# First loads of a four-block transformer kernel on three queues, with its written-out orders replaced

## The chip, the cores and the metric

The kernel runs on one core of a Trainium2 chip. The core has five engines that work side by side and wait for each other on semaphores: PE (TensorE, matrix products), DVE (VectorE), ACT (ScalarE), POOL (GpSimd) and SP (SyncE, which here only issues transfers). Transfers can be issued by SP, ACT and POOL, each through a queue of its own. The metric is the device time of one execution in microseconds (us). The kernel before takes 323.23 us, the median of three runs (323.01 to 323.62).

## The reference, cut to what matters

The input x has 2048 rows of 512 bf16 values. Two kinds of block alternate, A, B, A, B, each added to its input:

```
phi(t) = where(t > 0, t + 1, exp(t)) + 1e-6
A(x): y = layernorm(x);  q, k, v = y @ wqkv              # 32 heads of 16
      kv = sum over rows of phi(k)^T v ;  z = sum over rows of phi(k)
      o  = (phi(q) kv) / (phi(q) z + 1e-6) ;  return o @ wo
B(x): y = layernorm(layernorm(x))
      return gelu(y @ w1 + b1) @ w2 + b2                  # 512 -> 1792 -> 512
x = x + A(x);  x = x + B(x);  x = x + A(x);  x = x + B(x)
```

Because kv and z are sums over all rows, no output of a block A can be formed before every row has passed through its k product.

## The kernel before

The 2048 rows are 16 tiles of 128 rows, in four chunks of four. Operations carry names: layer (0 or 1), then tile or chunk. `K0_3` is the k product of tile 3 in layer 0 (four matmuls of 512 columns); `G0_3` adds (normalised x)^T phi(k) of that tile into four held PSUM banks; `Q0_0_2` is the q product for chunk 0; `Z` sums phi(k); `KV`, `M` and `WO` make the block's output; `W1x` and `W2x` are the two products of block B.

A tile passes through these steps in the first block A. DVE takes statistics (`statsA0_3`, `aggrA0_3`), POOL makes the inverse deviation (`vepsA0_3`, `powA0_3`, a power of -0.5), DVE or ACT normalises (`normA0_3`). The result is transposed so that PE can multiply it by the weights: by a transposing DMA on SP (`TA0_3`), or, for the tiles at the very start, by PE against an identity (`PTA0_3`) and a copy out of PSUM by ACT (`tcA0_3`). Tiles 0 and 1 use a shortened way: only the mean is taken off (`cenA0_0`), PE transposes that (`PTC0`, `tcC0`), and the missing scale is applied where ACT reads the k product (`expk0_0`, `reluk0_0`). Tile 3 gets its statistics from ACT (`sumA0_3`, `sqA0_3`, with a small step `negA0_3` on POOL). After the k product, ACT takes exp and relu of it, DVE a minimum (`mink0_0`) and a sum (`phik0_0`); that is phi(k).

Nothing is ordered by the hardware or a planner at run time. The table `CONF` (L241 to L606) holds for every engine the list of all its operations by name (`ORDER`), the buffer of every tile (`PLACES`), the engine of each operation that has a choice (`WAY`), the first loads (`LOADS`), and a train of matmuls on constants that PE plays while no data is there (`WARM`: seven of 512 columns in `warm0`, eight of 256 columns in `warm1` to `warm8`). Each engine plays its list strictly in order (L1306 to L1318). An operation that waits holds up all that is behind it on the same engine, transfers issued by that engine included. `ACT` loads its function table first (L1310).

The lists begin so (before):

```
sp:   x0 x1 wka wkc xc1 wq xc3 TA0_0 TA0_1 xc2 TA0_5 TA0_4 TA0_7 TA0_6 ...
act:  wkb wkd sumA0_3 tcC0 sqA0_3 tcC1 reluk0_0 tcA0_2 expk0_0 tcA0_3 expk0_1 reluk0_1 ...
pool: id0 neghalf bdm0 bdm1 id1 vepsA0_0 powA0_0 negA0_3 vepsA0_2 powA0_2 vepsA0_3 powA0_3 ...
dve:  ones statsA0_0 aggrA0_0 cenA0_0 statsA0_2 statsA0_1 ... normA0_2 statsA0_5 normA0_3 aggrA0_5 normA0_1 statsA0_4 mink0_0 ...
pe:   warm0 warm8 warm2 warm6 PTC0 warm1 warm7 warm5 warm4 warm3 K0_0a K0_0b PTC1 K0_0c K0_0d PTA0_2 K0_1 PTA0_3 K0_2 K0_3 G0_0_0 G0_1_0 Q0_0_2 ...
```

`x0` is tile 0 (128 KB), `x1` tiles 1 to 3 (384 KB), `xc1` to `xc3` the other chunks (512 KB each; `xc1` is issued only when `x0` has landed), `wka` to `wkd` the four quarters of the key weights (128 KB each; rows 0-127, 256-383, 128-255 and 384-511 are wka, wkb, wkc and wkd), `wq` the query weights (512 KB). `wkb` waits for `ones`, a DVE memset. `K0_0` is split in four matmuls, each needing one quarter of the key weights, in the order 2, 0, 3, 1 (`ks0`, used at L874 to L883). `bdm0`, `bdm1` and `id1` build a mask and the identity on POOL. The value weights and the weights of block B are issued by POOL much later (`wv`, `wo`, `w1_0` ... at L728), after all `TA0` transposes have landed.

Of the kernel before, what the change touches and what calls it, by code (L numbers as in the profile page):

```python
# [1359 lines left out]
```

## Time and profile before

| | |
|---|---|
| median of three runs | 323.23 us (323.01 to 323.62) |
| the profiled execution | 323.1 us, of which 321.9 us lie between its first and last instruction (the span) |
| PE busy | 318.0 us of the span, granted clock 1.00 |
| DVE, ACT, POOL busy | 218.1, 189.3 and 145.5 us |
| first transfer issued | 0.79 us after the start of the span |
| x0 landed, statistics of tile 0 begin | 3.25 us |
| last idle time of PE before the end | ends at 9.16 us |

Times in the text are us from the start of the span unless said otherwise. "Busy" for PE counts a matmul from its start until its result has drained, so a few tenths of waiting can hide inside a busy share; the starts in the timeline show them. A run of matmuls of 512 columns starts one every 0.216 us (four of them: 0.86 us). In the timeline a line is `start, duration, engine, source line, operation, out<-in, count`, and what stands in brackets is the engine's idle time before it and what ended it. A "q" behind an engine's name marks the transfers that it issues.

### The profile page before, as it was taken

Reading aid. Unit: us, or ns where it says so; the run is one execution under the profiler, and the core shown is the slowest. Engines: PE = TensorE matmul, PEld = TensorE weight load, DVE = VectorE, ACT = ScalarE, POOL = GpSimd, SP = SyncE. Lnnn points to the kernel's source line nnn. Section 1 sums busy time; section 2 is a strip of 40 time slices with the busy share of each in tenths; the row PEclk is TensorE's granted clock in tenths of the full one; section 3 lists DMA queues with packets and bytes.
Section 4 is the critical chain, followed back from the end, with each engine's and each line's share of the span. In section 5 each row is a group of like instructions: output and inputs, shape, how many; then the busy total and the mean of one; then the engine's idle time right before and its main releaser. Section 6 shows DMA issues by size and latency. Waiting matters only on the chain.

```text
span 321.9 us, 4748 instructions
## 1 busy us (share of the span) xinstructions
PE 318.0 (99%) x1703; PEld 157.4 (49%) x1703; DVE 218.1 (68%) x529; ACT 189.3 (59%) x324; POOL 145.5 (45%) x216
## 2 busy tenths in 40 slices
PE   8999999999999999999999999999999999999997
PEld 3444554666444444444444444558544444444444
DVE  5998789999786774028848899999889881101103
ACT  5898656797730636667962367979634442663320
POOL 6573978688655355101822415887454163000000
DMA  7844793142121412111010200122232322201002
GB/s 257 200 81 85 241 348 85 35 82 36 33 49 34 82 33 51 34 33 32 18 40 10 51 16 0 35 51 52 50 62 54 98 65 67 49 0 35 16 33 65
DMA packets 52355, 21.68 MB, mean 67 GB/s; under 512 B 47532, under 2 KB 50860, under 8 KB 52332
## 3 DMA queue, kind: packets, MB, share of 16 engines
q1 hardware_dynamic: 50844, 16.37, 22.4%
q0 software_dynamic: 1056, 4.72, 4.3%
q10 hardware_dynamic: 432, 0.30, 0.3%
q8 instruction: 13, 0.21, 0.3%
q14 instruction: 10, 0.08, 0.1%
HBM read 8.00 MB, written 2.10 MB: 31 GB/s over the span
## 4 chain that ended last, share of the span: by engine, by line
PE 97%; DMA 2%; DVE 0%; issue 0%
PE ps L1153 30%; PE ps L1190 29%; PE ps L1123 9%; PE ps L879 8%; PE ps L896 6%; PE ps L984 4%; PE ps L1013 4%; DMA t<-in_A_x_dram 2%; PE ps L909 2%; PE ps L1176 1%; PE ps L970 1%; PE ps L1034 1%; PE ps L1057 1%; PE ps L1100 1%; DVE stats L775 0%; PE ps L1048 0%
## 5 line engine op out<-in xcount | busy, mean ns | idle before, releaser
L1158 ACT ACTIVATE gT<-ps,b1c 128x512 bf16<-128x512 f32 (+1 forms) x140 | 77.0, 601 | 68.7 <-PE ps L1153 68.1
L1153 PE MATMUL ps<-t,w 128*128 128x512 bf16 (+1 forms) x560 | 102.5, 336 | 0.0
L1190 PE MATMUL ps<-w,gT 128*128 128x512 bf16 x434 | 98.6, 379 | 0.0
L1153 PEld LDWEIGHTS ps<-t,w 128*128 128x128 bf16 x560 | 54.8, 98 | 43.7 <-ACT gT L1158 0.2
L1190 PEld LDWEIGHTS ps<-w,gT 128*128 128x128 bf16 x434 | 42.5, 98 | 50.4
L784 POOL TENSOR_TENSOR rstd<-veps,neghalf 128x1 f32<-128x1 f32 x64 | 39.0, 625 | 41.1 <-DVE veps L782 38.9
L847 ACT ACTIVATE eb<-ps 128x512 bf16<-128x512 f32 x62 | 35.4, 606 | 19.3 <-PE ps L896 7.3
L1200 DVE TENSOR_TENSOR yb<-ps,xsb 128x512 bf16<-128x512 f32 x15 | 10.2, 688 | 41.4 <-PE ps L1190 41.4
L775 DVE BATCH_NORM_STATS2 stats<-xsb 128x6 f32<-128x512 f32 x48 | 32.0, 681 | 0.3
L1123 PE MATMUL ps<-gtb,t 128*128 128x512 bf16 x128 | 31.4, 379 | 0.0
L879 PE MATMUL ps<-wqkv,t 128*128 128x512 bf16 x128 | 30.9, 379 | 0.3 <-ACT t L835 0.3
L858 ACT ACTIVATE rb<-ps 128x512 bf16<-128x512 f32 x43 | 25.3, 607 | 5.8 <-PE ps L879 5.8
L798 ACT ACTIVATE yb<-xsb,nmr,rstd 128x512 bf16<-128x512 f32 x21 | 16.9, 814 | 15.1 <-POOL nmr L795 15.1
L896 PE MATMUL ps<-wqkv,t 128*128 128x512 bf16 x96 | 24.1, 379 | 0.0
L1089 POOL TENSOR_TENSOR t<-t,rr 128x512 bf16<-128x512 bf16 x18 | 19.3, 1072 | 9.0 <-DVE rr L1085 6.4
L782 POOL TENSOR_SCALAR veps<-mv 128x1 f32<-128x1 f32 x35 | 8.2, 236 | 32.7 <-DVE mv L777 31.3
L1196 DVE TENSOR_TENSOR xsb<-ps,xsb 128x512 f32<-128x512 f32 x16 | 10.8, 678 | 17.9 <-PE ps L1190 17.9
L1139 POOL TENSOR_TENSOR xsb<-xsb,b2b 128x512 f32<-128x512 f32 x17 | 21.4, 1267 | 3.0 <-DVE yb L803 2.9
L1077 POOL TENSOR_TENSOR lr<-t,zrow 128x512 f32<-128x512 bf16 x14 | 16.5, 1179 | 7.3 <-ACT zrow L997 4.5
L1123 PEld LDWEIGHTS ps<-gtb,t 128*128 128x128 bf16 x128 | 12.5, 98 | 14.5
L803 DVE TENSOR_SCALAR yb<-xsb,mv,rstd 128x512 bf16<-128x512 f32 x27 | 14.5, 542 | 7.3 <-POOL rstd L784 6.0
L879 PEld LDWEIGHTS ps<-wqkv,t 128*128 128x128 bf16 x128 | 12.1, 98 | 14.7 <-ACT t L835 0.9
(99 smaller groups left out, 363.7 us busy)
## 6 DMA issues: line engine op xcount, KB each, us to landing
w<-in_B_w_dram POOLq DMA_DIRECT2D x4, 896.0 KB, 9.1
out_dram<-yb SPq DMA_DIRECT2D x15, 128.0 KB, 2.0
t<-in_A_x_dram SPq DMA_DIRECT2D x3, 512.0 KB, 4.8
t<-yb SPq DMA_TRANSPOSE x62, 2.5
wqkv<-in_A_wqkv_dram SPq DMA_DIRECT2D x1, 512.0 KB, 5.9
wqkv<-in_A_wqkv_dram POOLq DMA_DIRECT2D x1, 512.0 KB, 4.7
wo<-in_A_wo_dram POOLq DMA_DIRECT2D x1, 512.0 KB, 5.3
t<-in_A_x_dram SPq DMA_DIRECT2D x1, 384.0 KB, 3.3
```

Source lines behind the costliest of these rows:

```text
L775: G.op("dve", lambda e: e.bn_stats(stats[:, s.slot, :], src()), 620, reads=src_keys, writes=[k + "s"], tiles=[s, *src_tiles], name=f"stats ...
L784: G.op("pool", lambda e: e.tensor_tensor(rstd[:, s.slot:s.slot + 1], veps[:, s.slot:s.slot + 1], neghalf[:], op=ALU.pow), 570, reads=[k + ...
L847: G.op("act", lambda e: e.activation(eb[:, et.slot, :], bank(bt), ACT.Exp, scale=by()), 478, reads=[src_key, *more_keys], writes=[f"e{tag} ...
L858: G.op("act", lambda e: e.activation(rb[:, rt.slot, :], bank(bt), ACT.Relu, scale=by()), 478, reads=[src_key, *more_keys], writes=[f"r{tag ...
L879: ins = e.matmul(bank(b), lhsT=yTa(yT)[:, dt, k * P:(k + 1) * P], rhs=wqkv[:, dt, D:2 * D], start=(i == 0 and n == 0), stop=(i == len(part ...
L896: ins = e.matmul(bank(b), lhsT=yTa(yT)[:, dt, k * P:(k + 1) * P], rhs=wqkv[:, dt, 0:D], start=(dt == 0), stop=(dt == DT - 1))
L1089: lambda e, d=d, tok=tok, heads=heads: e.tensor_tensor(heads(tok()), heads(tok()), rr[:, d.slot, :].unsqueeze(2).broadcast_to([P, H, DH]), ...
L1123: ins = e.matmul(bank(wb), lhsT=yTa(pq)[:, kt, k * P:(k + 1) * P], rhs=gtb[:, kt, :], start=(kt == 0), stop=(kt == DT - 1))
L1139: G.op("pool" if on_pool else "dve", lambda e: e.tensor_tensor(xsb[:, st, :], xsb[:, st, :], b2b[:], op=ALU.add), 1120 if on_pool else 600 ...
L1153: ins = e.matmul(bank(b, n), lhsT=w1[:, dt, ft * P:(ft + 1) * P], rhs=yTa(yT)[:, dt, k0 * P:k1 * P], start=(dt == 0), stop=(dt == DT - 1))
L1158: G.op("act", lambda e, ft=ft, b=b, k0=k0, k1=k1, n=n: e.activation(gT[:, g.slot, ft * 512 + k0 * P:ft * 512 + k1 * P], bank(b, n), ACT.Ge ...
L1190: ins = e.matmul(bank(b), lhsT=gT[:, g.slot, ft * 512 + k * P:ft * 512 + (k + 1) * P], rhs=w2[:, ft, :], start=(ft == 0), stop=(ft == FT - 1))
```

## The change

Three things change in `CONF`; the arithmetic, the number of operations on PE and their sizes stay, but for `K0_0`.

First, the loads. `x1` moves from SP to ACT, where it is the first instruction behind the table load and waits for nothing. The key weights come as three transfers: `wkb` (quarter 0, SP), `wka` (quarter 1, ACT) and `wkp` (quarters 2 and 3 in one transfer of 256 KB, POOL, between `id1` and `vepsA0_0`). `K0_0` is now three steps: `K0_0a` needs wkb, `K0_0b` needs wka, and `K0_0c`, two matmuls, needs wkp.

Second, the lists of all engines are new from the start to about the first block's output, and again in the second block A and the start of the second block B (`Q1_...` to `W11_0_...`). The middle and the tail are as before. Third, buffers are placed anew to fit (PSUM banks, `t4`, statistics slots), and seven small steps change engine: `b21_4` and `pr1_3_3` from POOL to DVE, `vepsA0_13` and `vepsB1_6` from POOL to DVE, `vepsB0_7`, `vepsB1_1` and `vepsB1_5` from DVE to POOL.

```diff
-    LOADS=[['x0', 'sp', 'x', 0, 0, 1, ''], ['x1', 'sp', 'x', 0, 1, 4, ''], ['wkb', 'act', 'wk', 0, 2, 3, 'ones'], ['wka', 'sp', 'wk', 0, 0, 1, ''], ['wkd', 'act', 'wk', 0, 3, 4, ''], ['wkc', 'sp', 'wk', 0, 1, 2, ''], ['xc1', 'sp', 'x', 1, 0, 4, 'x0'], ['wq', 'sp', 'wq', 0, 0, 4, ''], ['xc3', 'sp', 'x', 3, 0, 4, ''], ['xc2', 'sp', 'x', 2, 0, 4, '']],
+    LOADS=[['x0', 'sp', 'x', 0, 0, 1, ''], ['x1', 'act', 'x', 0, 1, 4, ''], ['wkb', 'sp', 'wk', 0, 0, 1, ''], ['wka', 'act', 'wk', 0, 1, 2, ''], ['wkp', 'pool', 'wk', 0, 2, 4, ''], ['xc1', 'sp', 'x', 1, 0, 4, 'x0'], ['wq', 'sp', 'wq', 0, 0, 4, ''], ['xc3', 'sp', 'x', 3, 0, 4, ''], ['xc2', 'sp', 'x', 2, 0, 4, '']],
         "sp":
-            "x0 x1 wka wkc xc1 wq xc3 TA0_0 TA0_1 xc2 TA0_5 TA0_4 TA0_7 TA0_6 TA0_13 TA0_14 TA0_15 TA0_12 TA0_8 TA0_10 TA0_9 "
+            "x0 wkb xc1 wq xc3 TA0_0 TA0_1 TA0_5 TA0_4 xc2 TA0_7 TA0_6 TA0_13 TA0_14 TA0_12 TA0_8 TA0_15 TA0_10 TA0_9 TA0_11 "
         "pe":
-            "warm0 warm8 warm2 warm6 PTC0 warm1 warm7 warm5 warm4 warm3 K0_0a K0_0b PTC1 K0_0c K0_0d PTA0_2 K0_1 PTA0_3 K0_2 "
-            "K0_3 G0_0_0 G0_1_0 Q0_0_2 Q0_0_1 Q0_0_0 K0_5 G0_2_0 K0_4 Z0_0 G0_3_0 Q0_1_0 K0_7 Q0_1_3 K0_6 G0_4_0 G0_5_0 "
+            "warm0 warm2 warm7 warm6 PTC0 warm4 warm3 warm1 warm5 K0_0a K0_0b warm8 PTC1 K0_0c PTA0_2 K0_1 PTA0_3 K0_2 G0_0_0 "
+            "K0_3 G0_1_0 Q0_0_2 Q0_0_1 Q0_0_0 K0_5 K0_4 G0_2_0 Q0_1_0 K0_7 G0_3_0 Q0_1_3 G0_4_0 Z0_0 K0_6 Q0_1_2 G0_5_0 K0_14 "
         "act":
-            "wkb wkd sumA0_3 tcC0 sqA0_3 tcC1 reluk0_0 tcA0_2 expk0_0 tcA0_3 expk0_1 reluk0_1 reluk0_3 expk0_2 reluk0_2 "
+            "x1 wka sumA0_3 tcC0 sqA0_3 tcC1 expk0_0 tcA0_2 reluk0_0 expk0_1 tcA0_3 reluk0_1 expk0_2 reluk0_3 reluk0_2 "
         "dve":
-            "statsA0_5 normA0_3 aggrA0_5 normA0_1 statsA0_4 mink0_0 aggrA0_4 phik0_0 mink0_1 normA0_5 phik0_1 statsA0_7 "
+            "statsA0_5 normA0_3 aggrA0_5 mink0_0 normA0_1 phik0_0 statsA0_4 mink0_1 aggrA0_4 normA0_5 phik0_1 statsA0_7 "
         "pool":
-            "id0 neghalf bdm0 bdm1 id1 vepsA0_0 powA0_0 negA0_3 vepsA0_2 powA0_2 vepsA0_3 powA0_3 powA0_1 vepsA0_5 powA0_5 "
+            "id0 neghalf eps6 bdm0 bdm1 id1 wkp vepsA0_0 negA0_3 powA0_0 b1z vepsA0_2 powA0_2 vepsA0_3 powA0_3 powA0_1 "
...
-            "nmrA0_10 vepsA0_9 powA0_9 nmrA0_11 phik0_14 eps6 wv wo phik0_8 w1_0 w1_1 w2_0 w2_1 phiq0_1_1 pr0_0_0 pz0_1_0 "
+            "vepsA0_9 nmrA0_10 nmrA0_11 powA0_9 phik0_14 wv phik0_8 wo phiq0_1_1 w1_0 w1_1 w2_0 w2_1 pr0_0_0 pz0_1_0 pr0_0_3 "
...
-        "den0_3": "tok", "den1_1": "tok", "den1_2": "tok", "den1_3": "tok", "ks0": "2|0|3|1", "normA0_0": "dve",
+        "den0_3": "tok", "den1_1": "tok", "den1_2": "tok", "den1_3": "tok", "ks0": "0|1|23", "normA0_0": "dve",
```

Functions gain the choice of other chunk orders (`CHUNKS`) and of a half-and-half way of the denominator (`by_half`, `load_half`); with the table as given the chunk order is 0, 1, 2, 3 everywhere and no entry asks for the half way, so these branches make the same instructions as before.

More of the change, by code (lines that the diff above doesn't have):

```diff
@@ L709, in load_w, with load_half @@
                                [f"{which}_{d}" for d in range(d0, d1)], name=name, kb=128 * (d1 - d0), after=after)
+        def load_half(name, queue, h, after):
+            G.parts[("x0", 0)] = (("x0", 0, 0), ("x0", 0, 1))
+            ps_ = slice(64 * h, 64 * h + 64)
+            loaded[name] = dma(queue, lambda e: e.dma_start(
+                t4[ps_, x0[0].slot, 0:D].rearrange("p (k d) -> p k d", k=1), rows(x_dram, 0)[ps_, 0:1, :]),
+                [("x0", 0, h)], [x0[0]], name=name, kb=64, after=after)
         for name, queue, what, at, lo, hi, behind in cf["LOADS"]:
             after = [loaded[b] for b in behind.split()]
-            if what == "x":
+            if what == "half":
+                load_half(name, queue, at, after)
+            elif what == "x":
                 load_x(name, queue, at, lo, hi, after)
@@ L751, in build_kernel, with by_token, by_half @@
             G.op("pe", warm, sum(cols) / 1.2, tiles=[wu], name=f"warm{n}", n=len(cols))
-        def by_token(L, c):
-            return eng(f"den{L}_{c}") == "tok"
+        def by_token(L, c, k=0):
+            way = eng(f"den{L}_{c}")
+            return way == "tok" or (way == "half" and k >= 2)
+        def by_half(L, c):
+            return eng(f"den{L}_{c}") == "half"
+        tokq = {}
         def norm(src, src_keys, src_tiles, double, on_act, tag, src16=False, head=False, centred=None):
@@ L862, in phi @@
             on_pool = eng(f"phi{tag}") == "pool"
             G.op("pool" if on_pool else "dve",
-                 lambda e: e.tensor_tensor(dst(), eb[:, et.slot, :], rb[:, rt.slot, :], op=ALU.add),
-                 1150 if on_pool else 338, reads=[f"e{tag}", f"r{tag}"], writes=[dst_key], tiles=[et, rt, *dst_tiles],
+                 lambda e: e.tensor_tensor(dst(), eb[:, et.slot, 0:n], rb[:, rt.slot, 0:n], op=ALU.add),
+                 (1150 if n == D else 580) if on_pool else (338 if n == D else 190), reads=[f"e{tag}", f"r{tag}"], writes=[dst_key], tiles=[et, rt, *dst_tiles],
@@ L887, in attn_q, with fn @@
         def attn_q(L, c, yT, pq):
-            if by_token(L, c):
-                for k in range(4):
+            half = by_half(L, c)
+            own = pq
+            if half:
+                own = tokq[(L, c)] = Tile(T4, f"pqt{L}_{c}")
+            n = 2 * P if half else 4 * P
+            if not by_token(L, c):
+                for kt in range(DT):
+                    b = Tile(psum, f"q{L}_{c}_{kt}" + "c" * half, "q")
+                    def fn(e, kt=kt, b=b):
+                        for dt in range(DT):
+                            ins = e.matmul(bank(b, n), lhsT=wqkv[:, dt, kt * P:(kt + 1) * P], rhs=yTa(yT)[:, dt, 0:n],
+                                           start=(dt == 0), stop=(dt == DT - 1))
+                        return ins
+                    G.op("pe", fn, 4 * MM if n == D else 4 * (n / 2.4 + 2.5), reads=[f"yT{L}_{4 * c + k}" for k in range(n // P)] + ["wq"], writes=[f"q{L}_{c}_{kt}" + "c" * half],
+                         tiles=[b, yT], name=f"Q{L}_{c}_{kt}" + "c" * half, lat=MM_DRAIN, n=4)
+                    phi(b, f"q{L}_{c}_{kt}" + "c" * half, lambda kt=kt: yTa(pq)[:, kt, 0:n], f"pq{L}_{c}_{kt}" + "c" * half, [pq], f"q{L}_{c}_{kt}" + "c" * half, n=n)
+            for k in range(4):
+                if by_token(L, c, k):
                     b = Tile(psum, f"q{L}_{c}_{k}", "q")
@@ L900, in attn_q, with attn_z @@
                          tiles=[b, yT], name=f"Q{L}_{c}_{k}", lat=MM_DRAIN, n=4)
-                    phi(b, f"q{L}_{c}_{k}", lambda k=k: t4[:, pq.slot, k * D:(k + 1) * D], f"pq{L}_{c}_{k}", [pq],
+                    phi(b, f"q{L}_{c}_{k}", lambda k=k: t4[:, own.slot, k * D:(k + 1) * D], f"pq{L}_{c}_{k}", [own],
                         f"q{L}_{c}_{k}")
-                return
-            for kt in range(DT):
-                b = Tile(psum, f"q{L}_{c}_{kt}", "q")
-                def fn(e, kt=kt, b=b):
-                    for dt in range(DT):
-                        ins = e.matmul(bank(b), lhsT=wqkv[:, dt, kt * P:(kt + 1) * P], rhs=yTa(yT)[:, dt, :],
-                                       start=(dt == 0), stop=(dt == DT - 1))
-                    return ins
-                G.op("pe", fn, 4 * MM, reads=[f"yT{L}_{4 * c + k}" for k in range(4)] + ["wq"], writes=[f"q{L}_{c}_{kt}"],
-                     tiles=[b, yT], name=f"Q{L}_{c}_{kt}", lat=MM_DRAIN, n=4)
-                phi(b, f"q{L}_{c}_{kt}", lambda kt=kt: yTa(pq)[:, kt, :], f"pq{L}_{c}_{kt}", [pq], f"q{L}_{c}_{kt}")
         zfirst = {}
-        def attn_z(L, c, pks):
-            by_sum = [int(v) for v in (eng("zc0") or "").split()] if L == 0 else list(range(NC - 1))
+        def attn_z(L, c, pks, order):
+            by_sum = [int(v) for v in (eng("zc0") or "").split()] if L == 0 else order[:NC - 1]
+            others = [v for v in order if v not in by_sum]
             def fold(add):
@@ L973, in attn_z, with attn_g_held @@
             G.op("pe", fn, 400, reads=[f"pk{L}_{4 * c + k}" for k in range(4)] + ["onesm"], writes=[f"zc{L}_{c}"], tiles=[b, *pks], name=f"Z{L}_{c}", lat=MM_DRAIN, n=16)
-            total(b, f"zc{L}_{c}", f"zs{L}_{c}", bool(L) or c != min(v for v in range(NC) if v not in by_sum))
-            if L == 0 and by_sum and c == max(v for v in range(NC) if v not in by_sum):
+            total(b, f"zc{L}_{c}", f"zs{L}_{c}", bool(L) or c != others[0])
+            if L == 0 and by_sum and c == others[-1]:
                 fold(True)
-        def attn_g_held(L, st, k, y, ykey, pk, gb):
-            parts = [(dc,) for dc in range(DT)] if st == ST - 1 else [tuple(range(DT))]
+        def attn_g_held(L, st, k, y, ykey, pk, gb, first, last):
+            parts = [(dc,) for dc in range(DT)] if last else [tuple(range(DT))]
             for part in parts:
@@ L984, in fn @@
                         ins = e.matmul(ps[:, gb.slot + dc, :], lhsT=yb[:, y.slot, dc * P:(dc + 1) * P], rhs=pkb[:, pk.slot, :],
-                                       start=(st == 0), stop=(st == ST - 1))
+                                       start=first, stop=last)
                     return ins
                 keys = [f"g{L}_{dc}" for dc in part]
-                G.op("pe", fn, len(part) * MM, reads=[ykey, f"pk{L}_{st}"] + (keys if st else []), writes=keys,
+                G.op("pe", fn, len(part) * MM, reads=[ykey, f"pk{L}_{st}"] + ([] if first else keys), writes=keys,
                      tiles=[y, pk, gb], name=f"G{L}_{st}_{part[0]}", lat=MM_DRAIN, n=len(part))
@@ L1004, in attn_g_out, with attn_g_chunk @@
                 copy(gtb[:, dc, :], gb, f"g{L}_{dc}", ("gt", dc), dc % 2, f"g{L}_{dc}", off=dc)
-        def attn_g_chunk(L, c, ys, ykeys, pks):
+        def attn_g_chunk(L, c, ys, ykeys, pks, first, last):
             for dc in range(DT):
@@ L1017, in attn_g_chunk @@
                      tiles=[b, *ys, *pks], name=f"G{L}_{c}_{dc}", lat=MM_DRAIN, n=4)
[L1018 removed]
+                if first:
                     G.op("dve", lambda e, dc=dc, b=b: e.tensor_scalar(gacc[:, dc, :], bank(b), 1.0, None, op0=ALU.mult), 600,
                          reads=[f"g{L}_{c}_{dc}"], writes=[("gacc", dc)], tiles=[b], name=f"ga{L}_{c}_{dc}", lat=40)
[L1021 removed]
+                elif not last:
                     G.op("dve", lambda e, dc=dc, b=b: e.tensor_tensor(gacc[:, dc, :], bank(b), gacc[:, dc, :], op=ALU.add), 600,
@@ L1042, in attn_kv @@
                  reads=["zs", "bdmask"], writes=["zb"], name=f"zb{L}", lat=40, fast=True)
-            if any(by_token(L, c) for c in range(NC)):
+            if any(by_token(L, c, 3) for c in range(NC)):
                 zr = Tile(psum, f"zr{L}", "t")
@@ new lines, in attn_den @@
+            half = by_half(L, c)
+            src = tokq[(L, c)] if half else pq
+            pt = pq if half or not by_token(L, c) else Tile(T4, f"pt{L}_{c}")
+            n = 2 * P if half else 4 * P
+            if not by_token(L, c):
+                for kt in range(DT):
+                    tag = f"{L}_{c}_{kt}" + "c" * half
+                    b = Tile(psum, f"d{tag}", "n")
+                    r = Tile(LR, f"lr{tag}")
+                    key = f"pq{L}_{c}_{kt}" + "c" * half
+                    G.op("pe", lambda e, kt=kt, b=b: e.matmul(bank(b, n), lhsT=zb[:, kt * P:(kt + 1) * P], rhs=yTa(pq)[:, kt, 0:n], start=True, stop=True),
+                         MM if n == D else n / 2.4 + 2.5, reads=[key, "zb"], writes=[f"d{tag}"], tiles=[b, pq], name=f"D{tag}", lat=MM_DRAIN)
+                    G.op("act", lambda e, b=b, r=r: e.activation(lr[:, r.slot, 0:n], bank(b, n), ACT.Ln, bias=eps6[:]), 575 if n == D else 362,
+                         reads=[f"d{tag}", "eps6"], writes=[f"l{tag}"], tiles=[b, r], name=f"ln{tag}", lat=90, table="exp")
+                    G.op("act", lambda e, r=r: e.activation(lr[:, r.slot, 0:n], lr[:, r.slot, 0:n], ACT.Exp, scale=-1.0), 536 if n == D else 323,
+                         reads=[f"l{tag}"], writes=[f"l{tag}"], tiles=[r], name=f"rec{tag}", lat=110, table="exp")
@@ L1093, in attn_den @@
-                    dma("sp", lambda e, k=k, tok=tok: e.dma_start_transpose(yTa(pt)[:, :, k * P:(k + 1) * P], tok()), [f"pt{tag}"],
-                        tiles=[pq, pt], reads=[f"pq{tag}"], name=f"TP{tag}", sem=("pT", pq, k), transpose=True)
-                return pt
-            for kt in range(DT):
-                b = Tile(psum, f"d{L}_{c}_{kt}", "n")
-                r = Tile(LR, f"lr{L}_{c}_{kt}")
-                tag = f"{L}_{c}_{kt}"
-                G.op("pe", lambda e, kt=kt, b=b: e.matmul(bank(b), lhsT=zb[:, kt * P:(kt + 1) * P], rhs=yTa(pq)[:, kt, :], start=True, stop=True),
-                     MM, reads=[f"pq{tag}", "zb"], writes=[f"d{tag}"], tiles=[b, pq], name=f"D{tag}", lat=MM_DRAIN)
-                G.op("act", lambda e, b=b, r=r: e.activation(lr[:, r.slot, :], bank(b), ACT.Ln, bias=eps6[:]), 575,
-                     reads=[f"d{tag}", "eps6"], writes=[f"l{tag}"], tiles=[b, r], name=f"ln{tag}", lat=90, table="exp")
-                G.op("act", lambda e, r=r: e.activation(lr[:, r.slot, :], lr[:, r.slot, :], ACT.Exp, scale=-1.0), 536,
-                     reads=[f"l{tag}"], writes=[f"l{tag}"], tiles=[r], name=f"rec{tag}", lat=110, table="exp")
+                         lambda e, kt=kt, r=r: e.tensor_tensor(yTa(pq)[:, kt, 0:n], yTa(pq)[:, kt, 0:n], lr[:, r.slot, 0:n], op=ALU.mult),
@@ new lines, in attn_den, with tok, heads @@
+                         (1150 if on_pool else 600) if n == D else (580 if on_pool else 330),
+                         reads=[f"l{tag}", key], writes=[key], tiles=[r, pq], name=f"pr{tag}", lat=40,
+                         fast=not on_pool)
+            for k in range(4):
+                if not by_token(L, c, k):
+                    continue
+                tag = f"{L}_{c}_{k}"
+                r = Tile(LR, f"lr{tag}")
+                d = Tile(RD, f"rd{tag}")
+                def tok(k=k):
+                    return t4[:, src.slot, k * D:(k + 1) * D]
+                def heads(ap):
+                    return ap.rearrange("p (h x) -> p h x", x=DH)
+                on_pool = eng(f"pz{tag}") != "dve"
+                G.op("pool" if on_pool else "dve",
+                     lambda e, r=r, tok=tok: e.tensor_tensor(lr[:, r.slot, :], tok(), zrow[:], op=ALU.mult), 1150 if on_pool else 600,
+                     reads=[f"pq{tag}", "zrow"], writes=[f"l{tag}"], tiles=[r, src], name=f"pz{tag}", lat=60,
+                     fast=not on_pool)
+                G.op("dve", lambda e, r=r, d=d, heads=heads: e.tensor_reduce(rd[:, d.slot, :], heads(lr[:, r.slot, :]),
+                                                                              mybir.AxisListType.X, ALU.add), 600,
+                     reads=[f"l{tag}"], writes=[f"rd{tag}"], tiles=[r, d], name=f"red{tag}", lat=60)
+                G.op("dve", lambda e, d=d: e.tensor_scalar(rd[:, d.slot, :], rd[:, d.slot, :], 1e-6, None, op0=ALU.add), 100,
+                     reads=[f"rd{tag}"], writes=[f"rd{tag}"], tiles=[d], name=f"den{tag}", lat=60)
+                G.op("dve", lambda e, d=d: e.reciprocal(rr[:, d.slot, :], rd[:, d.slot, :]), 300,
+                     reads=[f"rd{tag}"], writes=[f"rr{tag}"], tiles=[d], name=f"rec{tag}", lat=60)
@@ new lines, in attn_den, with attn_out @@
+                     1150 if on_pool else 600, reads=[f"rr{tag}", f"pq{tag}"], writes=[f"pq{tag}"], tiles=[d, src],
+                     name=f"pr{tag}", lat=60, fast=not on_pool)
+                dma("sp", lambda e, k=k, tok=tok: e.dma_start_transpose(yTa(pt)[:, :, k * P:(k + 1) * P], tok()), [f"pt{tag}"],
+                    tiles=[src, pt], reads=[f"pq{tag}"], name=f"TP{tag}", sem=("pT", src, k), transpose=True)
+            return pt
+        def attn_out(L, c, k, pq, base, base_keys, base_tiles, first):
@@ L1116, in attn_out @@
             st = 4 * c + k
             wb = Tile(psum, f"wo{L}_{st}", "w")
-            parts = [(kt,) for kt in range(DT)] if st == 0 else [tuple(range(DT))]
+            parts = [(kt,) for kt in range(DT)] if first else [tuple(range(DT))]
             for part in parts:
@@ L1124, in wfn @@
                     return ins
-                G.op("pe", wfn, len(part) * MM, reads=([f"pt{L}_{c}_{k}"] if by_token(L, c) else [f"pq{L}_{c}_{kt}" for kt in part]) + [("gt", kt) for kt in part]
+                G.op("pe", wfn, len(part) * MM, reads=([f"pt{L}_{c}_{k}"] if by_token(L, c, k) else [f"pq{L}_{c}_{kt}" + "c" * by_half(L, c) for kt in part]) + [("gt", kt) for kt in part]
                      + ([f"wo{L}_{st}"] if part[0] else []), writes=[f"wo{L}_{st}"], tiles=[wb, pq],
@@ L1141, in mlp_front, with mlp_up @@
                  fast=not on_pool)
-        def mlp_up(L, c, yT, g):
-            parts = [(0, 2), (2, 4)] if c == 0 else [(0, 4)]
+        def mlp_up(L, c, yT, g, first):
+            parts = [(0, 2), (2, 4)] if first else [(0, 4)]
             for hf, (k0, k1) in enumerate(parts):
@@ L1206, in build_kernel @@
         gb = Tile(psum, "g4", "g4", 4)
-        pq1, trs = [], []
-        for c in range(NC):
+        pq1, trs = {}, []
+        orders = cf["CHUNKS"]
+        for c in orders[0]:
             yT = Tile(T4, f"yT0_{c}")
             pq = Tile(T4, f"pq0_{c}")
-            pq1.append(pq)
+            pq1[c] = pq
             pks = []
@@ L1252, in build_kernel @@
         for L in range(2):
-            nxt = []
-            for c in range(NC):
+            nxt = {}
+            chunks = orders[1 + L]
+            for c in chunks:
                 yT = Tile(T4, f"yBT{L}_{c}")
```

68 lines of the change are left out of this document (19 added, 49 removed), and 308 rows, old and new, of tables (ORDER, PLACES, WAY).

## The prediction

> **What bounds the kernel now.** I read the page's busy line first, then the chain of work that ended last in order of time, then the timelines of single engines over the first 14 us, and last the transfers that POOL issues later in the run. The page:
>
> ```profile
> PE 318.0 (99%) x1703; PEld 157.4 (49%) x1703; DVE 218.1 (68%) x529; ACT 189.3 (59%) x324; POOL 145.5 (45%) x216
> ```
>
> PE is busy for all but 3.9 us, so only work of PE or waits of PE can move the time. The chain's first 20 us (start, length, what):
>
> ```profile
> 0.79 2.44 DMA t<-in_A_x_dram
> 3.23 0.02 issue
> 3.24 4.83 DMA t<-in_A_x_dram
> 8.07 0.02 issue
> 8.09 0.69 DVE stats L775
> 8.79 0.33 DVE yb L803
> 9.12 0.04 issue
> 9.16 0.40 PE ps L825 x4
> 9.56 1.73 PE ps L879 x8
> ```
>
> Two loads in a row set the start: x0 lands at 3.23, xc1 is issued then and lands at 8.07, DVE stands at `statsA0_5` until it does, and `normA0_3` behind it lets `PTA0_3` start at 9.16. From there to 319.94 the chain is PE alone, pieces end to end. So nothing after 9.16 can be won, only lost, and the head is worth what PE idles there. PE's own timeline:
>
> ```profile
> 5.86 0.60 PE L879 MATMUL ps<-wqkv,t 128*128 128x512 bf16 x2 [0.30 <-ACT t L835]
> 6.55 0.40 PE L825 MATMUL ps<-idp,yb 128*128 128x128 bf16 x4
> 6.78 0.59 PE L879 MATMUL ps<-wqkv,t 128*128 128x512 bf16 x2
> 7.43 0.40 PE L825 MATMUL ps<-idp,yb 128*128 128x128 bf16 x4
> 7.67 1.03 PE L879 MATMUL ps<-wqkv,t 128*128 128x512 bf16 x4
> 9.16 0.40 PE L825 MATMUL ps<-idp,yb 128*128 128x128 bf16 x4 [0.47 <-DVE yb L803]
> ```
>
> These are K0_0a/b, PTC1, K0_0c/d, PTA0_2, K0_1, PTA0_3. The largest hole, from the end of K0_1's stream (7.67 + 4 x 0.216 = 8.53) to 9.16, is 0.63; the others are 0.30 and two under 0.1. About 1.0 us is all that the head holds from 5.86 on.
>
> **The change part by part.**
>
> *x0, x1, wkb, wka.* SP's first four issues (two rows of two, 0.87 and 0.90 us) become two. This frees nothing: xc1 still waits for x0. x1's issue moves from about 1.25 to between 0.80 (the table load's start) and 1.48 (ACT's first issue before, which waited for `ones`). x1 landed 3.3 us after its issue, at about 4.6. Bounds: 0.45 earlier, or 0.4 later if it shares the engines with x0 and wkb. x0 now has x1 beside it; 384 KB at 358 to 387 GB/s (the windows from 2.8 to 3.5) are 1.0 us, so x0 lands between 0 and 1.0 later. I take x0 +0.4, x1 -0.1, nearer to the small end since the windows from 1.8 to 2.4 ran at 92 to 215 GB/s and had room. Both are hidden: K0_0a/b end near 6.9 instead of 6.46, PTC1 near 7.3, and the next step waits longer, as follows. The cover is gone if x0 is over 0.7 late.
>
> *wkp on POOL, the new wait.* K0_0c now needs a transfer that POOL issues behind `id1`. POOL's rows, and POOL's first transfer (issued at 32.54; the second line is its size and time to landing):
>
> ```profile
> 3.25 0.29 POOL L720 TENSOR_SCALAR_AFFINE_SELECT idp<-idp 128x128 bf16<-128x128 bf16 x1
> 32.54 0.97 POOL L728 DMA_DIRECT2D wqkv<-in_A_wqkv_dram  x1
> ```
> ```profile
> wqkv<-in_A_wqkv_dram POOLq DMA_DIRECT2D x1, 512.0 KB, 4.7
> ```
>
> `bdm0` cannot start before `ones` (1.45), and with bdm1 and id1 behind it wkp goes out at 3.55. wkp is half of that transfer's size; the full rate was 418 GB/s (35.5 to 36.0), so 256 KB less is 0.63 us less: 4.07, landing 7.6. It shares the engines with xc1, which no POOL transfer before did that early; I add 0.2. Ends: 2.8 (x0's 2.4, an SP row on idle engines, plus 128 KB at 0.35 MB/us), landing 6.35; and 5.3 (`wo`, 512 KB queued behind `wv`), landing 8.85. I take T = 7.8, since the row of the same queue and tensor is nearest.
>
> *What is queued behind that wait.* On PE all of PTA0_2, K0_1, PTA0_3, K0_2. On ACT `expk0_0` stands ahead of `tcA0_2`, which K0_2 needs. Two matmuls 0.43 and a start 0.02: T + 0.45. ACT started 0.27 after the last K0_0 stream before (6.78 + 0.43 = 7.21, next ACT row 7.48), then 0.57 to the next ACT row (7.48 to 8.05), tcA0_2 0.60, release 0.05: K0_2 at T + 1.94. On PE alone it would be T + 0.45 + 0.24 + 0.86 + 0.24 = T + 1.79, so ACT decides. Before, K0_2 was at 9.56. Then `G0_0_0` is pulled ahead of K0_3 and needs `phik0_0`: reluk0_0 starts 0.48 after tcA0_2 and takes 0.68 (T + 2.45), phik0_0 0.43, release 0.1: T + 3.0, while K0_2 ends at T + 2.80: a new hole of 0.2. After it K0_3 and G0_1_0 find their inputs (tcA0_3 ends at T + 3.45, phik0_1 about T + 4.45, needed at T + 4.73). So the train arrives at the old place when T = 9.56 - 1.94 - 0.2 = 7.4, and each 0.1 later costs 0.1. At T = 7.8: +0.4.
>
> *xc1, POOL's small steps.* SP's queue ahead of xc1 falls from 768 to 256 KB; 0 to 1.5 us (512 KB at 350 GB/s) earlier in itself, less x0's 0.4 and wkp's share. I take 7.4 (ends 6.6 and 8.5). POOL issues wkp for 0.97 in the 0.71 us in which it idled, takes negA0_3 before powA0_0, and b1z (0.2): `powA0_3` ends near 8.25 instead of 7.9. normA0_3 then ends at 8.7, PTA0_3 needs it at T + 1.55 = 9.35. Hidden, 0.65 to spare; gone if xc1 lands after 8.2 or T is under 7.15.
>
> *xc2 behind TA0_5 and TA0_4.* SP issued xc2 at 10.76 (3.8 us to land). Now it follows TA0_4, whose normA0_4 I put at 13.6 (DVE is one 0.69 statistics behind, as phik0_0 comes first): TA0_4 1.2, xc2 at 14.9, landing 18.7, and TA0_7 behind it near 19.2 (TA0_5 landed 0.6 after xc2 before). K0_7 moves up: before it now stand three Q0_0, K0_5, K0_4, G0_2_0, Q0_1_0, so 13.42 + 7 x 0.86 = 19.45. Hidden with 0.25 to spare; TA0_0's 4.6 us in place of 3.7 would cost 0.65. In return TA0_5 and TA0_4 have no load ahead of them, worth nothing since K0_5 had them in time (PE had no hole).
>
> *The other new lists.* The last TA0 transposes leave SP one every 1.3 us, as before; K0_11 has about 1 us to spare. POOL's `wv` and `wo` are now apart, one or two 1.15 us sums later; KV0 reads wv near 47, ten after its landing. In the second block A, POOL's rows end at 205.73 and WO1_0 starts at 205.79: no slack, but the names up to there are unchanged. pr1_3_3 and b21_4 go to DVE, 0.7 each in place of 1.06 and 1.2 on POOL, which idled 2.8 us before 229.7. All of these: 0 to +0.7 each (one DVE row). I take 0.
>
> Sum against the profiled 323.1 (span 321.9 and 1.2 around it): +0.4, 323.5. The median of the runs stands 0.13 above that execution, so 323.6 as a median. What a measurement of this kernel can tell from no change is about 0.2%, 0.65 us; this forecast is within it.
>
> **The rivals.**
>
> *A, wkp late (slower).* Place: K0_0c. It decides above T = 8.05. At `wo`'s 5.3 us, T = 8.85: +1.45, 324.7. For it: `wv` moved 103 and 74 GB/s in the two half microseconds after its first bytes at 34.0. Against: part of that may be the queue's first use after a pause, already in the 4.7. [...]
>
> *B, wkp early (faster).* At T = 6.35 normA0_3 decides: PTA0_3 at 8.75, K0_2 at 8.98, no hole before G0_0_0: -0.6, 322.6. For it: wkp's tensor is being read by wka and wkb already. [...]
>
> *C, a later list waits (slower).* K0_7 waits for TA0_7 behind xc2, +0.65 on top of +0.4: 324.3. For it: 0.25 to spare against transposes that took 2.4 to 4.6. Against: K0_7 itself slides later with every delay ahead of it.
>
> *D, x1 lands no earlier.* x1's start is hidden under T, so 323.6 all the same; it counts to the likeliest.
>
> **How the numbers follow.** Likeliest (with D): 0.50, 323.6, its own range 323.1 to 323.9. A 0.17, C 0.18, B 0.15. B reaches 0.2% only if powA0_3 is early too, so of its 0.15 I count 0.12 as faster; A and C both end slower by more than that: 0.35; the rest, 0.53, is within 0.2%. The range 322.7 to 324.9 leaves out most of B and the upper end of A together with C.
>
> **What would show it.** Right: PE stands before K0_0c until about 7.8, the first ACT row after it is an exp, K0_2 starts near 9.75, a hole of some 0.2 before the first L984 matmuls, then no hole to the end. Wrong: K0_0c before 7.2 or after 8.3; the chain leading through x0 and xc1 again; a wait of PE for a transpose between 19 and 34; a hole of PE between 205 and 232; matmuls of 512 columns spaced above 0.216 us after the longer wait.

## The result and the profile after

The changed kernel takes 324.38 us, the median of six executions (324.21 to 324.96); the kernel before takes 323.42 us, also the median of six (322.84 to 323.64). The ratio is 1.0035, with a 95% interval from 1.0022 to 1.0048: slower by 0.7 to 1.6 us. The forecast of 323.6 had this inside its range, but its likeliest case, within 0.2%, is not what came. The profiled execution has a span of 323.1 us, 1.2 us above that of before. The page's busy line:

```profile
PE 316.8 (98%) x1673; PEld 157.6 (49%) x1703; DVE 220.0 (68%) x530; ACT 189.6 (59%) x324; POOL 142.5 (44%) x216
```

Thirty records of PE are missing here, so the busy sums can't be compared; the starts of PE's matmuls can. The chain of work that ended last, first 11 us (start, length, what):

```profile
0.97 0.50 DVE onesm L699
...
1.53 0.87 POOL bdmask L741
...
2.46 0.85 POOL bdmask L744
...
3.51 4.55 DMA wqkv<-in_A_wqkv_dram
8.06 0.05 issue
8.11 0.60 PE ps L895 x2
8.72 0.22 PE ps L841 x4
8.94 0.86 PE ps L895 x4
9.80 0.22 PE ps L841 x4
10.03 1.00 PE ps L895 x4
11.02 1.04 PE ps L1005 x4
```

x0 and xc1 no longer lead. The head now hangs on `ones`, `bdm0`, `bdm1`, `id1` and behind them wkp, issued at 3.51, landing at 8.06. PE's timeline (L895 is the k product, L1005 the G product, L1149 the WO product):

```profile
8.11 0.60 PE L895 MATMUL ps<-wqkv,t 128*128 128x512 bf16 x2 [0.77 <-DMA wqkv<-in_A_wqkv_dram]
9.99 1.04 PE L895 MATMUL ps<-wqkv,t 128*128 128x512 bf16 x4
11.02 1.04 PE L1005 MATMUL ps<-pkb,yb 128*128 128x512 bf16 x4
253.71 1.02 PE L1149 MATMUL ps<-gtb,t 128*128 128x512 bf16 x4 [0.40 <-DMA t<-t]
```

The first three are K0_0c, K0_2 and G0_0_0. The first Q0_0_2 starts at 13.62, where it started at 12.85 before: 0.77 lost in the head. PE then runs without a hole to 253, where WO1_11 waits for a transpose. In starts, its stream is 0.56 late there (the 0.40 in brackets counts from the drained result of the matmul ahead). 0.77 + 0.56 = 1.33; PE's last matmul starts at 321.02, 1.32 after the 319.70 of before. So the whole loss has two places, 240 us apart, and the second is far from anything that the loads touch.

What makes WO1_11's transpose late stands on DVE and POOL near 244. First before, then after (L1077 and L1120 are the same operation `pz1_2_3`; L1139 and L1165 are POOL's add `b21_7`):

```profile
243.55 0.69 DVE L1077 TENSOR_TENSOR lr<-t,zrow 128x512 f32<-128x512 bf16 x1
243.64 0.73 POOL L795 TENSOR_SCALAR nmr<-mv,rstd 128x1 f32<-128x1 f32 x1
244.33 1.15 POOL L1139 TENSOR_TENSOR xsb<-xsb,b2b 128x512 f32<-128x512 f32 x1
```
```profile
244.31 1.68 DVE L1120 TENSOR_TENSOR lr<-t,zrow 128x512 f32<-128x512 bf16 x1
244.29 1.16 POOL L1165 TENSOR_TENSOR xsb<-xsb,b2b 128x512 f32<-128x512 f32 x1
```

Before, DVE's operation was under way first and took 0.69, and POOL's small `nmrB1_13` beside it was stretched from its usual 0.27 to 0.73. After, POOL's add starts 0.02 ahead of DVE's operation, and DVE's takes 1.68: it ends at 245.99, 0.54 after the add. In both executions the one that is first holds the other up. DVE then reaches the reduction, the reciprocal and the product behind it 1 us late, and the transpose that WO1_11 reads is issued at 251.19.

### The profile page after: what moved, and what is told of

It is laid out like the page before. It is cut to its first block, busy times and chain, and to the rows that moved or that the text cites. A ratio compares the mean times of both kernels' runs of the same rounds, so it can differ in the third digit from the quotient of the medians.

```text
span 323.1 us, 4718 instructions
## 1 busy us (share of the span) xinstructions
PE 316.8 (98%) x1673; PEld 157.6 (49%) x1703; DVE 220.0 (68%) x530; ACT 189.6 (59%) x324; POOL 142.5 (44%) x216
## 4 chain that ended last, share of the span: by engine, by line
PE 86%; DVE 9%; DMA 2%; POOL 1%; issue 1%; ACT 0%
PE ps L1216 28%; PE ps L1179 24%; PE ps L895 9%; PE ps L1149 6%; PE ps L928 5%; PE ps L1005 4%; PE ps L1034 4%; PE ps L916 2%; DVE xsb L1154 2%; DVE stats L791 2%; DMA wqkv<-in_A_wqkv_dram 1%; DVE rd L1123 1%; PE ps L1202 1%; DVE lr L1120 1%; DMA t<-t 1%
## 5 line engine op out<-in xcount | busy, mean ns | idle before, releaser
L895 PE MATMUL ps<-wqkv,t 128*128 128x512 bf16 x125 | 30.4, 379 | 1.3 <-DMA wqkv<-in_A_wqkv_dram 0.8
L1149 PE MATMUL ps<-gtb,t 128*128 128x512 bf16 x123 | 30.8, 379 | 0.6 <-DMA t<-t 0.4
L814 ACT ACTIVATE yb<-xsb,nmr,rstd 128x512 bf16<-128x512 f32 x21 | 17.0, 814 | 13.0 <-POOL nmr L811 12.9
L1132 POOL TENSOR_TENSOR t<-t,rr 128x512 bf16<-128x512 bf16 x17 | 17.9, 1061 | 13.9 <-DVE rr L1128 11.2
L928 PE MATMUL ps<-wqkv,t 128*128 128x512 bf16 x94 | 23.7, 379 | 0.1
L798 POOL TENSOR_SCALAR veps<-mv 128x1 f32<-128x1 f32 x36 | 9.4, 260 | 32.2 <-DVE mv L793 30.2
L1165 POOL TENSOR_TENSOR xsb<-xsb,b2b 128x512 f32<-128x512 f32 x16 | 20.2, 1270 | 3.4 <-DVE yb L819 2.3
L1120 POOL TENSOR_TENSOR lr<-t,zrow 128x512 f32<-128x512 bf16 x14 | 16.3, 1161 | 9.9 <-ACT zrow L1018 4.5
L1149 PEld LDWEIGHTS ps<-gtb,t 128*128 128x128 bf16 x128 | 12.5, 98 | 15.1 <-issue 0.9
L895 PEld LDWEIGHTS ps<-wqkv,t 128*128 128x128 bf16 x128 | 12.1, 98 | 15.3 <-DMA wqkv<-in_A_wqkv_dram 0.9
L876 DVE TENSOR_SCALAR eb<-eb 128x512 bf16<-128x512 bf16 x45 | 14.6, 331 | 7.0 <-ACT eb L863 6.9
```

Of the source, the lines that this page charges most:

```text
L895: ins = e.matmul(bank(b), lhsT=yTa(yT)[:, dt, k * P:(k + 1) * P], rhs=wqkv[:, dt, D:2 * D], start=(i == 0 and n == 0), stop=(i == len(part ...
L928: ins = e.matmul(bank(b), lhsT=yTa(yT)[:, dt, k * P:(k + 1) * P], rhs=wqkv[:, dt, 0:D], start=(dt == 0), stop=(dt == DT - 1))
L1120: lambda e, r=r, tok=tok: e.tensor_tensor(lr[:, r.slot, :], tok(), zrow[:], op=ALU.mult), 1150 if on_pool else 600,
L1149: ins = e.matmul(bank(wb), lhsT=yTa(pq)[:, kt, k * P:(k + 1) * P], rhs=gtb[:, kt, :], start=(kt == 0), stop=(kt == DT - 1))
L1165: G.op("pool" if on_pool else "dve", lambda e: e.tensor_tensor(xsb[:, st, :], xsb[:, st, :], b2b[:], op=ALU.add), 1120 if on_pool else 600 ...
```

## The experiments

Theory L held that the head loses because wkp is issued late, behind the mask; Q that a POOL transfer costs by what it takes from others. For the second place, C held that POOL's add holds DVE up, S that SP's new order does it. Later names stand in the expectations. Times are medians; "before" is the kernel before, run beside each group on the same chip, 323.42 to 323.57 us.

| run | time | ratio, 95% interval | first Q0_0_2 | lost ahead of W10_0 | lost near 253 |
|---|---|---|---|---|---|
| before | 323.42 to 323.57 | | 12.85 | 0 | 0 |
| changed | 324.38 | 1.0035 [1.0022, 1.0048] | 13.62 | 0 | 0.56 |
| wkp first | 324.27 | 1.0032 [1.0019, 1.0044] | 12.93 | 0 | 0.57 |
| wkp on ACT | 323.99 | 1.0020 [1.0006, 1.0035] | 13.01 | 0.72 | 0.56 |
| add earlier | 324.18 | 1.0028 [1.0016, 1.0041] | 13.37 | 0 | 0 |
| before, x1 on ACT | 324.12 | 1.0014 [1.0001, 1.0028] | 12.94 | 1.01 | 0 |
| before, wk on POOL | 328.03 | 1.0130 [1.0096, 1.0165] | 16.16 | 0.71 | 0 |
| both moved | 323.63 | 1.0004 [0.9988, 1.0020] | 13.22 | 0.83 | 0 |
| both, x1 behind x0 | 324.05 | 1.0016 [0.9994, 1.0037] | 12.65 | 0 | 0 |
| before, wk first on POOL | 323.74 | 1.0004 [0.9985, 1.0024] | 12.44 | 0.62 | 0 |
| changed, again | 324.97 | 1.0041 [1.0024, 1.0057] | 14.25 | 0 | 0.56 |
| add earlier, again | 323.76 | 1.0012 [0.9997, 1.0026] | 13.88 | 0 | 0 |

The last three columns are starts and missing stream of PE in the profiled execution of each. A median holds eight to twelve executions of a run (six of the changed kernel and of "wk on POOL"), and executions of one kernel lie up to 3.4 us apart, so an effect of some tenths is read from the columns. The columns explain the one profiled execution, and that need not lie near the median: it took 323.58 us with the add earlier (median 324.18), 324.27 with both moved (323.63) and 322.86 with x1 behind x0 (324.05).

**wkp first on POOL** (changed kernel):

```diff
-id0 neghalf eps6 bdm0 bdm1 id1 wkp vepsA0_0
+id0 neghalf eps6 wkp id1 bdm0 bdm1 vepsA0_0
```

> The changed kernel with one name moved: POOL issues wkp ahead of id1, bdm0 and bdm1. Theory L (the head's loss is a late issue): wkp goes out near 1.0 instead of 3.51, takes about the same 4.55 us and lands near 5.5; K0_0c follows PTC1 near 7.2 without a wait; then powA0_3 and normA0_3 decide, PTA0_3 at 8.7, K0_2 near 9.1 (9.99 in the changed kernel), the first Q0_0_2 near 12.7 (13.62; before the change 12.85). Time 324.4 - 0.9 = 323.5, and 323.1 if the later loss of 0.4 goes too. Rival Q (POOL's transfer costs by what it takes from the others): x0 and x1 land 0.5 or more later, all of the head with them, and the time stays at 324.0 or above.

wkp goes out at 1.40 and lands at 5.62, after 4.23 us, and the wait ahead of K0_0c is gone (7.21). x0 lands at 3.80 and x1 at 4.19, as in the changed kernel, so Q is refuted in its form. But xc1 lands at 8.16 instead of 7.37, and PTA0_3 starts at 9.24, not 8.7. The chain of work leads through x0 and xc1 again:

```profile
0.80 3.00 DMA t<-in_A_x_dram
3.80 0.02 issue
3.82 4.34 DMA t<-in_A_x_dram
```

The head is 0.69 better than the change and 0.08 worse than before: L has the cause of the wait and overrates the gain. The median, 324.27, is where Q had it and hardly shows the gain; the profiled execution, 323.74, is the third fastest of its twelve. The loss near 253 is unchanged, though the head is back in its place:

```profile
243.62 1.68 DVE L1120 TENSOR_TENSOR lr<-t,zrow 128x512 f32<-128x512 bf16 x1
```

So the late head does not make the collision; both engines moved together.

**wkp on ACT** (changed kernel):

```diff
-['wkp', 'pool', 'wk', 0, 2, 4, '']
+['wkp', 'act', 'wk', 0, 2, 4, '']
-act: x1 wka sumA0_3
+act: x1 wka wkp sumA0_3
```

> The changed kernel with wkp issued by ScalarE behind wka instead of by POOL; all else stays. Theory L: wkp goes out near 1.7, lands near 5.3, and the head is that of the run with wkp first on POOL to within 0.2 us: K0_2 near 9.1, 323.1 to 323.5. Rival Q: without a POOL transfer the head is better than that run's by 0.5 us or more, under 322.9 where that one stays at 324.

wkp goes out at 1.73, lands at 5.95, and Q0_0_2 starts at 13.01, 0.08 from the run with POOL. For wkp's own time to landing the route did not matter (4.22 us after 4.23). The heads agree for different reasons, though. Here xc1 lands at 7.22, 3.16 us after its issue, and holds nothing up; x0 lands at 4.04, 0.81 later than before the change, and the chain goes from x0 straight to PE:

```profile
0.80 3.24 DMA t<-in_A_x_dram
4.04 0.02 issue
4.06 0.70 DVE stats L791
```

So the agreement is in part a coincidence. Q's better head did not come, and L's 323.1 to 323.5 is missed too: W10_0 waits (0.72), and the loss near 253 is still there.

**The add earlier** (changed kernel):

```diff
-b21_1 pr1_2_2 powB1_13 nmrB1_13 b21_7 vepsB1_14
+b21_1 b21_7 pr1_2_2 powB1_13 nmrB1_13 vepsB1_14
```

> The changed kernel with one name moved: POOL's add b21_7 goes ahead of pr1_2_2, so that it no longer starts 0.02 us before DVE's pz1_2_3. Theory C (the later 0.4 us is DVE's bf16 operation held up while POOL's add runs): pz1_2_3 takes 0.69 instead of 1.68, PE has no wait of 0.40 for a transpose near 253.3, and the time is 324.4 - 0.4 = 324.0. Rival S (the order of the transposes on SP makes that wait): pz1_2_3 may get shorter, but WO1_11's wait stays within 0.1 of 0.40 and the time at 324.4.

DVE's operation is back to 0.69, and PE has no wait near 253:

```profile
244.06 0.69 DVE L1120 TENSOR_TENSOR lr<-t,zrow 128x512 f32<-128x512 bf16 x1
```

C holds, S falls: SP's list was not touched. In the median the step is small here (324.18); the pair at the end of this section settles it.

**x1 on ACT alone** (kernel before):

```diff
-sp: x0 x1 wka wkc xc1
-act: wkb wkd sumA0_3
+sp: x0 wka wkc xc1
+act: x1 wkb wkd sumA0_3
```

> The kernel before with one part of the change alone: x1 issued by ScalarE ahead of wkb and wkd. Theory L: this is the half of the change that helps: xc1 has 384 KB less ahead of it on its queue and lands near 7.4 instead of 8.07, x0 lands about 0.5 later as in the changed kernel, powA0_3 and normA0_3 decide, PTA0_3 near 8.7 (9.16), K0_2 near 8.95 (9.39): 323.4 - 0.45 = 322.95. Rival (the prediction's reading that x1's place changes nothing): 323.4, within 0.2.

L is wrong here, and the head is nearly where the prediction's reading puts it: xc1 lands at 7.75 instead of 8.07, but x0 at 3.94 instead of 3.23, since x1's 384 KB now start in the same moment. DVE and POOL begin tile 0 by 0.7 later, and PTA0_3 starts at 9.10 against 9.16. The first Q0_0_2 is 0.09 late. The time, 324.12, misses the rival's 323.4 as well (0.14% over before); in the profiled execution 1.01 us is lost at another place:

```profile
61.55 5.85 PE L1153 MATMUL ps<-t,w 128*128 128x256 bf16 x52 [0.84 <-DMA t<-yb]
```

This is W10_0 waiting for TB0_1, a transpose that took 4.40 us where it took 2.48 before; the last section tells what held it.

**Key weights on POOL alone** (kernel before):

```diff
-['wkb', 'act', 'wk', 0, 2, 3, 'ones'], ['wka', 'sp', 'wk', 0, 0, 1, ''], ['wkd', 'act', 'wk', 0, 3, 4, ''], ['wkc', 'sp', 'wk', 0, 1, 2, '']
+['wkb', 'sp', 'wk', 0, 0, 1, ''], ['wka', 'act', 'wk', 0, 1, 2, 'ones'], ['wkp', 'pool', 'wk', 0, 2, 4, '']
-"ks0": "2|0|3|1"
+"ks0": "0|1|23"
```

> The kernel before with one part of the change alone: key-weight quarters 2 and 3 as one POOL transfer behind id1, quarter 0 on SP behind x1, quarter 1 on ScalarE; x1 stays on SP and all other lists stay. Theory N (the head's loss is the POOL transfer, the later loss comes from the new lists of the second layer): x0 lands at 3.2 to 3.3 again, wkp at 7.8 to 8.1, K0_2 1.92 later at 9.7 to 10.0, the first Q0_0_2 at 13.2 to 13.45 (12.85 before the change, 13.62 with it), no wait of PE near 253; time 323.5 + 0.35 to 0.6 = 323.85 to 324.1. Rival V (any head that is this late moves DVE into POOL's add): the wait near 253 is there too, 0.5 more, 324.4 to 324.6.

Both expectations miss by 4 us. x0 lands at 3.27, so xc1, wq and xc3 go out earlier than in the changed kernel, xc1 even ahead of wkp; xc1 lands at 6.82 and wkp, behind them, at 9.26. It took 5.76 us. PE stands 2.43 us ahead of K0_0c, and then its clock falls. The second fence is a stretch of 2 us; its last three columns are the granted clock, the busy share of the DMA engines and GB/s:

```profile
9.31 1.03 PE L879 MATMUL ps<-wqkv,t 128*128 128x512 bf16 x2 [2.43 <-DMA wqkv<-in_A_wqkv_dram]
```
```profile
10.00:12.00 2.00, 2.00 (x9) 1.03 (x8) 0.00 (x0) 1.62 (x3) 0.00 (x0) 0.50 0.92 159
```

The four matmuls of K0_1 take 1.71 (10.56 to PTA0_3 at 12.27) instead of 0.86. So the two parts of the change seem to be tied: x1 on ACT delays x0 (3.76 in the changed kernel, 3.27 here), x0 delays SP's loads (xc1 issued at 3.78 there, behind wkp's 3.51), and that leaves the engines to wkp (4.55 us there). This is argued from the order of the issues; no run moves xc1 alone. By itself, the POOL transfer was far dearer. V falls: there is no loss near 253 with before's lists, though this head is 3.3 late.

**Both moved** (changed kernel, wkp first and the add earlier):

```diff
-id0 neghalf eps6 bdm0 bdm1 id1 wkp ... b21_1 pr1_2_2 powB1_13 nmrB1_13 b21_7
+id0 neghalf eps6 wkp id1 bdm0 bdm1 ... b21_1 b21_7 pr1_2_2 powB1_13 nmrB1_13
```

> The changed kernel with both names moved: wkp first on POOL and b21_7 ahead of pr1_2_2. Theory N: the first Q0_0_2 at 12.9, pz1_2_3 takes 0.69, no wait near 253, PE's last matmul within 0.15 of its place before the change, time 323.5 to 323.7. Rival W (the other new lists cost something of their own that is not seen yet): time 324.0 or above, with a wait of PE in a third place.

1.0004 [0.9988, 1.0020]: with the two causes gone the change is back at the time of before, and W's 324.0 is not reached (323.63), though the interval leaves room for 0.2%. The profiled execution agrees less well. pz1_2_3 takes 0.69 and nothing is lost near 253, but xc1 lands at 8.44, Q0_0_2 starts at 13.22, not 12.9, and W10_0 loses 0.83 to a late TB0_1, so PE's last matmul comes 1.2 after that of before, not within 0.15.

**Both moved, x1 behind x0**:

```diff
-sp: x0 wkb xc1          act: x1 wka sumA0_3
+sp: x0 x1 xc1           act: wkb wka sumA0_3   (wkb behind ones)
```

> As the kernel with both names moved, and x1 goes back to SP behind x0, with xc1 right behind it; the two single quarters of the key weights go out on ScalarE behind ones. Theory N with x0 as the start of the chain: x0 lands at 3.25 instead of 3.8, xc1 near 7.7, PTA0_3 near 8.85, the first Q0_0_2 near 12.55, 0.3 earlier than before the change; time 323.2. Rival T (PE only waits later what it gains here): the head is that early, but W10_0 waits near 60.5 for a transpose of normB, time 323.5 or above.

x0 lands at 3.21, xc1 at 7.77, PTA0_3 starts at 8.86, Q0_0_2 at 12.65: the head gains 0.20 against before, as x0's part of the theory says, and the profiled execution has no wait to its end (its last matmul starts at 319.50). The median, 324.05, does not show it, and T's wait is not in that execution either. What the others met was not seen.

**Before, with two quarters first on POOL**:

```diff
-sp: x0 x1 wka wkc xc1            pool: id0 neghalf bdm0 bdm1 id1
+sp: x0 x1 xc1                    pool: id0 neghalf wka id1 bdm0 bdm1   (wka: quarters 0 and 1)
-"ks0": "2|0|3|1"
+"ks0": "2|3|01"
```

> The kernel before, with the two quarters of the key weights that SP issued (0 and 1) as one POOL transfer ahead of id1, so that xc1 has only x1 ahead of it on SP. Theory N: xc1 lands near 7.5 instead of 8.07, PTA0_3 near 8.7 (9.16), K0_2 near 8.95 (9.39), the first Q0_0_2 near 12.4; time 323.05. Rival T: the head is that early, but the gain is lost in a wait near 60.5, time 323.5 or above.

xc1 lands at 7.55, PTA0_3 starts at 8.63, Q0_0_2 at 12.44: 0.41 gained. T holds: W10_0 waits at 60.68 for a TB0_1 of 4.01 us and gives 0.62 back; 323.74, not to be told from before. None of these versions beats it.

**The changed kernel and the earlier add, once more on one chip**:

> The changed kernel once more, unaltered, for more executions on one chip with the kernel below. Theory N: 324.4, wkp lands between 7.8 and 8.1, the first Q0_0_2 between 13.4 and 13.65, pz1_2_3 takes 1.68 again and PE loses 0.56 near 253, since what places these two operations is the same. Rival J (the collision was one execution's chance): pz1_2_3 takes 0.69 this time.

> The changed kernel with b21_7 ahead of pr1_2_2 once more, beside the unaltered one. Theory N: 0.4 to 0.6 under it in the median, since the wait near 253 is 0.56 of PE's stream; no wait of PE near 253. Rival J: the two medians within 0.15 of each other.

The collision is there again (1.68 at 244.95, the add at 244.92, 0.56 lost) and gone again with the add moved (0.69). The medians are 324.97 and 323.76. They differ by 1.2, twice the 0.56 and more than the 0.4 to 0.6 expected. Part of the rest stands in the head of the unaltered kernel's execution, 0.37 later than the other's: its first Q0_0_2 starts at 14.25, not between 13.4 and 13.65. It did not wait for wkp (7.88, K0_0c at 8.29), but PE's matmuls ran at half their rate until 9.5 (K0_0c took 1.06, in the other 0.60), a third way to lose. The late x0 is not the reason, for it lands at 4.14 in both executions. J falls.

## Why the prediction was right or wrong

**x0, x1, xc1, xc2, TA0_7: right.** x0 landed 0.53 late (forecast 0.4), x1 0.43 early (0.1, bound 0.45), xc1 at 7.37 (7.4), xc2 issued at 14.86 (14.9), TA0_7 landed at 19.11 (19.2). K0_7 started at 19.67 without a wait, so rival C did not come. x1 did land earlier than D had it, and it stays out of the chain, as D had it; no run moves x1's landing by itself, since in the run with x1 on ACT alone x0 moves too.

**wkp's landing: the mechanism right, the size 0.27 short.** Issue at 3.51 (3.55), but 4.55 us for 256 KB instead of 4.25, so T = 8.07 in place of 7.8. By the forecast's own sum that is the point (8.05) from which rival A decides. Over the runs the same transfer (256 KB on POOL) took 4.23 to 5.76.

**Behind the wait: right, but for its reference.** K0_2 came at T + 1.92 (forecast T + 1.94), G0_0_0 at T + 2.95 (T + 3.0), the hole before it 0.17 (0.2). The three executions in which wkp decides give T = 7.80, 8.07 and 8.32, and Q0_0_2 at 13.37, 13.62 and 13.88: the slope of 0.1 for each 0.1 is shown, and break-even is T = 12.85 - 5.56 = 7.3, not 7.4. The step that failed is "before, K0_2 was at 9.56". That is the chain's figure, which starts a piece where the one ahead has ended; the same matmuls start at 9.39 in PE's timeline, from which T + 1.94 was made. Two clocks were mixed, for 0.17. The forecast does so in two more places, without harm: the holes that it puts at "two under 0.1" are 0.25 and 0.21 in starts, and WO1_0 starts at 205.62, not 205.79. The head's 0.77 is 0.4 + 0.27 + 0.17 less some hundredths.

**"The other new lists ... I take 0": wrong, 0.56.** This is the other half of the loss, and the bound of 0.7 held it. The whole range, to 324.9, was left wide for rivals A and C and not for this, so that the result lies inside it is in part luck. The signs of being wrong look for such a hole between 205 and 232; it came at 253. The reason given for the 0.7, that DVE takes over 0.7 us operations, is not what happened. DVE reaches the reciprocal that releases POOL's pr1_2_2 earlier against PE: pr1_2_2 is 0.43 later than before, pz1_2_3, which follows a PE product, 0.76. That puts b21_7 just ahead of pz1_2_3. The run with wkp first shows that it is the lists and not the late head, those with the add earlier that it is this pair. Which of the new entries moved the reciprocal stays open. I had looked there for slack and load, not for which of two engines comes first. What makes the two hold each other up was not shown; what it costs was: 1.68 and 0.69 for the same operation.

**Rival B: its premise fails.** With wkp at 5.62, earlier than B's 6.35, the head gains nothing on before (12.93), because xc1 then lands at 8.16 and not 7.4. Why xc1 is late there stays open. That wkp's bytes push it back does not explain it: between 4 and 7 us SP's queue moved 0.57 MB in that run and 0.53 MB in the changed kernel, and with wkp on ACT, nearly as early, xc1 landed at 7.22. **The half that was thought to help, taken alone**, did not: neither x1 on ACT nor an early wkp with it beats the old head (12.94, 12.93 and 13.01 against 12.85).

## What to carry to other kernels

Put a load that PE waits for at the head of its queue (wkp landed at 5.62 there, at 8.06 behind the mask), and compare all landings of the same microseconds: in these runs moving one load forward often moved another back, x0 by 0.5 to 0.9 when x1 started beside it. When an order is written anew, look for pairs of DVE and POOL operations that meet within a few hundredths, since here that decided whether one operation of DVE took 0.69 or 1.68. And take both ends of a difference from one view of the profile.
